# A planner that knows of overlapping VectorE and GpSimd work: a new order for the first block of an H3 and MLP kernel

## The chip, the cores and the metric

The kernel runs on one core of one Trainium2 chip. A core has five engines that run side by side, each with its own queue of instructions, worked off in order: TensorE (PE in the profile; PEld is its weight load), VectorE (DVE), ScalarE (ACT), GpSimd (POOL) and SyncE (SP), which here issues the DMA transfers. Engines wait for one another through semaphores. The metric is the time of one execution on the device in microseconds (us).

## The reference

Two layers of the kind "long convolution, then MLP", both with the same weights, on 2048 tokens of 1024 features. Cut to what is computed:

```python
kv = k_shift * v                      # k_shift: causal convolution of k with 4 taps per channel
kv_f = rfft(pad(kv, 2 * S))           # long causal convolution with ssm_k, by channel
y = irfft(kv_f * rfft(pad(ssm_k)))[:S] + kv * ssm_D
A(q) = q * y
B(x) = square(relu(x @ w1 + b1)) @ w2 + b2      # 1024 -> 3584 -> 1024

x = q
x = x + A(layernorm(x)); x = x + B(layernorm(x))
x = x + A(layernorm(x)); x = x + B(layernorm(x))
```

All is float32. The convolution's result y doesn't depend on x, so it is made once and used in both layers.

## The kernel before, in words

Tokens are cut into four blocks of 512, the convolution into blocks of 256 tokens, which are transformed with tables by TensorE. The frequency products of a block are multiplied element by element, on GpSimd and VectorE, and transformed back. The MLP runs over (layer, block) units in the order of ORDER; every matmul with the weights is made as three matmuls of a high and a low part.

The kernel has two parts. `first_block()` (L932) makes all that the first MLP unit needs, for block 0: for each of 8 groups of 128 channels (c = 0 to 7) the short convolution of k and the product with v (`x_part`, L989), the transform of the filter (`g_part`, L1030), the products and the back transform for the two halves of the block (`prods`, L1127, jj = 0 and 1), the two layer norms (`ln_part`, `tail`), and the first eight weight pieces (`weight`, L1211). What comes after it, from `prod_stream` on, is the steady part: a hand-written loop of MLP steps, into which the convolution of the later blocks is mixed. The change doesn't touch it.

In `first_block` nothing is issued at once. Each operation is a task of a `Plan` (L86): the engines that can take it with a cost in ns for each (`opts`), what it reads and writes, and a latency. `Plan.run` (L177) draws PLAN_TRIES (L42) sets of priorities, the first six plain, then half of them with random factors, the rest as variations of the best so far. For each, `Plan.order` (L124) lays the tasks one after the other on a list of engines: among the tasks that are ready it takes the one that can start earliest, on the engine on which it would end earliest, and it adds that up to an end time. The order with the lowest end time is issued. So the costs decide two things: the order of the instructions on each engine, and, for tasks with two options, which of VectorE (V) and GpSimd (G) takes them.

Tasks with both options are the elementwise ones with inputs in SBUF: the product of the short convolution with v (L997), the frequency products (L1135 for jj = 0, L1140 for jj = 1, with the sum L1142 behind it), the combinations L1146 and L1147, the butterfly (L1149, issued at L655 and L656), the addition to x (L1172), and the low part of a weight (L1218). VectorE alone takes the three remaining steps of the short convolution (L994, a scalar_tensor_tensor), the evictions of transforms from PSUM (L1015, L1054, L1056, L1164, L1207), and the statistics (L1076 to L1096); the normalizations (L1107, L1110) go to VectorE or ScalarE. ScalarE copies the other transforms out. Costs before are straight lines of the number n of elements per partition:

```python
v_cost(n) = 130 + 1.04 * n      # VectorE, no rival on GpSimd
v2_cost(n) = 250 + 1.3 * n      # VectorE, for the tasks that GpSimd could take; +100, +150 or +400 at places
g_cost(n) = 200 + 2.45 * n      # GpSimd
```

Of the kernel before, what the change touches and what calls it, by code (L numbers as in the profile page):

```python
# [19 lines left out]
P = 128  # L20
T = 512
# [6 lines left out]
BL = 256  # L28
# [10 lines left out]
PAIR_GAP = 10  # L39
FWD_WAIT = 4  # L40
PLAN_H = (0.6, 0.7, 0.8, 0.85, 0.9, 0.95)
PLAN_TRIES = 400  # L42
NORM_0 = "VA"
AHEAD_0 = 4
BURST = 1.06
# [40 lines left out]
class Plan:  # L86
# [37 lines left out]
    def order(self, rise, noise):  # L124

        n = len(self.tasks)
        prio = [t[5] - rise * h * z + (1 - rise) * 1000 * i for i, (t, h, z) in enumerate(zip(self.tasks, self.height, noise))]
        waits = [len(t[2]) for t in self.tasks]
        made, left_users = set(), {}
        last = {}  # L130
        for t in self.tasks:
            for x in t[3]:
                left_users[x] = left_users.get(x, 0) + 1
        end, free, seq = [0.0] * n, {}, []
        at = [0.0] * n
        ready = [i for i in range(n) if not waits[i]]
        while ready:
            best = None
            for i in ready:
                opts, _, _, bufs, lat, _ = self.tasks[i]  # L140
                t = at[i]
                ok = True
                for x in bufs:
                    if x not in made:
                        if x.after is not None and x.after not in made or x.prev is not None and left_users[x.prev]:
                            ok = False
                            break
                        if x.prev is not None and last[x.prev] > t:
                            t = last[x.prev]
                if not ok:  # L150
                    continue
                f = None
                for e, c in opts:
                    st = max(t, free.get(e, 0.0))
                    if f is None or st + c < f:
                        f, pick = st + c, (e, c, st)
                key = (pick[2], prio[i])
                if best is None or key < best[0]:
                    best = key, i, pick
            _, i, (e, c, st) = best  # L160
            _, _, _, bufs, lat, _ = self.tasks[i]
            free[e] = st + c
            end[i] = st + c + lat
            for x in bufs:
                made.add(x)
                left_users[x] -= 1
                last[x] = max(last.get(x, 0.0), end[i])
            seq.append((i, e))
            ready.remove(i)
            for j in self.after[i]:  # L170
                waits[j] -= 1
                at[j] = max(at[j], end[i])
                if not waits[j]:
                    ready.append(j)
        return max(end), seq

    def run(self):  # L177
        n = len(self.tasks)
        self.height = [0] * n
        self.after = [[] for _ in range(n)]  # L180
        for i in reversed(range(n)):
            opts, _, deps, _, lat, _ = self.tasks[i]
            self.height[i] += min(c for _, c in opts) + lat
            for d in deps:
                self.height[d] = max(self.height[d], self.height[i])
                self.after[d].append(i)
        rng = np.random.default_rng(1)
        best = None
        for k in range(PLAN_TRIES):
            if k < len(PLAN_H):  # L190
                rise, noise = PLAN_H[k], np.ones(n)
            elif k < PLAN_TRIES // 2:
                rise, noise = PLAN_H[k % len(PLAN_H)], rng.uniform(0.85, 1.15, n)
            else:
                rise, noise = best[2], best[3] * np.where(rng.random(n) < 0.1, rng.uniform(0.7, 1.4, n), 1.0)
            got = self.order(rise, noise.tolist())
            if best is None or got[0] < best[0]:
                best = (*got, rise, noise)
        for i, e in best[1]:
            _, fn, _, bufs, _, _ = self.tasks[i]  # L200
            for x in bufs:
                if x.t is None:
                    x.t = x.make()
            fn(e)
        return best[0]
# [3 lines left out]
    return 130 + 1.04 * n  # L209


def v2_cost(n):
    return 250 + 1.3 * n


def g_cost(n):
    return 200 + 2.45 * n


def a_cost(n):  # L220
# [4 lines left out]
def tile_h3_mlp(ctx: ExitStack, tc: tile.TileContext, q, kT, vT, shk, ssmT, ssmD, w1, b1, w2, b2,  # L225
                fwd_t, pro_t, inv_t, sgn_t, out):
    nc = tc.nc
    V, A, G, PE, SY = nc.vector, nc.scalar, nc.gpsimd, nc.tensor, nc.sync
    ENG = {"V": V, "G": G}
# [702 lines left out]
    def first_block():  # L932
        b = ORDER[0][1]
        pl = Plan()
# [21 lines left out]
        with tc.tile_pool(name="pro", bufs=1) as pro:  # L956
# [32 lines left out]
            def x_part(c, k4, v4):  # L989
                ks = new(cv, "fx", 4, [P, T])  # L990
                pl.add([("A", a_cost(T))], lambda e: A.activation(
                    ks.t, k4.t[:, 3:], AF.Copy, scale=shkt[:, c, 0:1]), [k4], [ks])
                for q_ in range(1, 4):
                    pl.add([("V", v2_cost(T))], lambda e, q_=q_: V.scalar_tensor_tensor(  # L994
                        ks.t, k4.t[:, 3 - q_:T + 3 - q_], shkt[:, c, q_:q_ + 1], ks.t,
                        op0=OP.mult, op1=OP.add), [k4], [ks], lat=130)
                pl.add([("G", g_cost(T)), ("V", v2_cost(T))], lambda e: ENG[e].tensor_mul(  # L997
                    ks.t, ks.t, v4.t), [v4], [ks])
                o = bank("p2", 4, ps2)
                pl.add([("PE", 480)], lambda e: transposes(o.t, ks.t), [ks], [o])  # L1000
                xt = new(cv, "fg", 3, [P, T])
                pl.add([("A", a_cost(T))], lambda e: A.copy(xt.t, o.t), [o], [xt])
                sp = spec["x", c]
                for r in range(2):
                    oi = bank("p2", 4, ps2)

                    def mm(e, r=r, oi=oi):
                        for u in range(2):
                            ou = oi.t[:, u * BL:u * BL + BL]
                            fmm(ou, even(r), xt.t[:, 0:BL], True, False)  # L1010
                            fmm(ou, odd(r, u), xt.t[:, BL:], False, True)
                    pl.add([("PE", 1850)], mm, [xt, *tabs], [oi])
                    pl.add([("A", a_cost(T))], lambda e, r=r, oi=oi: A.copy(spread(sp[r].t), sums(oi.t)), [oi], [sp[r]])
                    if r:
                        pl.add([("V", v_cost(T))], lambda e, oi=oi: V.tensor_add(  # L1015
                            spread(sp[2].t), sums(oi.t), spread(sp[0].t)), [oi, sp[0]], [sp[2]])
                for i in range(3):
                    dma(lambda i=i: dview(XD[i], 0, c), lambda i=i: sp[i].t, [sp[i]])
# [108 lines left out]
            def prods(c, jj):  # L1127
                sm = new(cv, "sm", 2, [P, 3, 2, CU])
                xs, gs = spec["x", c], spec["g", c]
                n = BL * (jj + 1)  # L1130
                for ty, (xi, gi) in enumerate(PAIRS):
                    xt, gt = xs[xi], gs[gi]
                    opts = [("G", g_cost(n)), ("V", v2_cost(n) + 150)]
                    if jj == 0:
                        pl.add(opts, lambda e, ty=ty, xt=xt, gt=gt: ENG[e].tensor_mul(  # L1135
                            sm.t[:, ty], xt.t[:, :, 0], gt.t[:, :, 0]), [xt, gt], [(sm, ty)])
# [1 line left out]
                    pr = new(cv, "fx", 4, [P, T]) if c == KT - 1 else sub("ppr", 3, 512, [P, T], "xl")  # L1138
                    pv = lambda t: t.rearrange("p (g b c) -> p g b c", g=2, b=BT)
                    pl.add(opts, lambda e, xt=xt, gt=gt, pr=pr: ENG[e].tensor_mul(  # L1140
                        pv(pr.t), xt.t, gt.t[:, :, ::-1]), [xt, gt], [pr])
                    pl.add([("V", v2_cost(BL) + 100), ("G", g_cost(BL))], lambda e, ty=ty, pr=pr: ENG[e].tensor_add(  # L1142
                        sm.t[:, ty], pv(pr.t)[:, :, 0], pv(pr.t)[:, :, 1]), [pr], [(sm, ty)])
                two = [("G", g_cost(BL)), ("V", v2_cost(BL) + 100)]
                fl_ = lambda: sm.t.rearrange("p k g c -> p k (g c)")
                pl.add(two, lambda e: ENG[e].tensor_add(fl_()[:, 1], fl_()[:, 0], fl_()[:, 1]), [(sm, 0)], [(sm, 1)])  # L1146
                pl.add(two, lambda e: ENG[e].tensor_sub(fl_()[:, 2], fl_()[:, 0], fl_()[:, 2]), [(sm, 0)], [(sm, 2)])  # L1147
                z = {}
                pl.add([("V", 2 * v2_cost(BL) + 400), ("G", 2 * g_cost(BL))], lambda e: z.update(  # L1149
                    enumerate(butterfly(ENG[e], fl_()))), [], [(sm, 0), (sm, 1), (sm, 2)])  # L1150
                o = bank("pt", 2, pst)

# [9 lines left out]
                for e_ in range(2):  # L1162
                    tt = 2 * jj + e_
# [5 lines left out]
                dma(lambda: YD[0][:, 2 * jj:2 * jj + 2, sl], lambda: yo.t.rearrange("p (e c) -> p e c", e=2), [yo], cost=400)  # L1169
                for e_ in range(2):  # L1170
                    tt = 2 * jj + e_
                    pl.add([("G", g_cost(P)), ("V", v2_cost(P))], lambda e, e_=e_, tt=tt: ENG[e].tensor_add(  # L1172
                        x1[tt].t[:, sl], x1[tt].t[:, sl], yn.t[:, e_]), [(yn, e_)], [(x1[tt], c)])

            tails = {}
# [35 lines left out]
            def weight(w):  # L1211
                _, c, f, kh = wsrc[w]
# [2 lines left out]
                hi, lo = (hl, 0), (hl, 1)  # L1215
                dma(lambda: raw.t, lambda: w1[c * FC + f, :, 4 * kh:4 * kh + 4], w=[raw])
                pl.add([("A", a_cost(512))], lambda e: A.copy(hl.t[:, 0], raw.t), [raw], [hi])
                pl.add([("V", v2_cost(512)), ("G", g_cost(512))], lambda e: ENG[e].tensor_sub(  # L1218
                    hl.t[:, 1], raw.t, hl.t[:, 0].bitcast(F32)), [raw, hi], [lo])
                o = bank("p2", 4, ps2) if kh == 0 else rs[c, f]["b"]  # L1220
                if kh == 0:
# [42 lines left out]
        n = 2 * AHEAD_0  # L1264
# [340 lines left out]
```

## Time and profile before

| | |
|---|---|
| median of 3 runs | 2829.53 us (2827.84 to 2832.18) |
| profiled execution | 2825.19 us |
| its span | 2823.4 us |
| granted TensorE clock, mean | 0.990 |
| DVE busy share in the first 3 of 40 slices | 8, 8, 6 tenths |
| POOL busy share in the first 3 of 40 slices | 6, 8, 2 tenths |
| DMA | 711.71 MB, mean 252 GB/s |

The page cuts the span into 40 slices of 70.6 us; the first block fills the first two. The table of PE's slices has a 7 and an 8 there and 9 in nearly all that follow:

```profile
PE   7899899799999999999999999999999999999999
PEld 6787788688888888888888888888888888888887
DVE  8868688767777877779757654252225322352122
ACT  4254244242334333442234322242224222342222
POOL 6826555345442655336552553001000100001000
```

Each digit is the busy share of a slice in tenths. An instruction that has started counts as busy until it ends, also while it is held up by another engine's use of the memory; so a full DVE or POOL row doesn't say that the engine works all that time.

### The profile page before, as it was taken

Reading aid. Unit: us, or ns where it says so; the run is one execution under the profiler, and the core shown is the slowest. Engines: PE = TensorE matmul, PEld = TensorE weight load, DVE = VectorE, ACT = ScalarE, POOL = GpSimd, SP = SyncE. Lnnn points to the kernel's source line nnn. Section 1 sums busy time; section 2 is a strip of 40 time slices with the busy share of each in tenths; the row PEclk is TensorE's granted clock in tenths of the full one; section 3 lists DMA queues with packets and bytes.
Section 4 is the critical chain, followed back from the end, with each engine's and each line's share of the span. In section 5 each row is a group of like instructions: output and inputs, shape, how many; then the busy total and the mean of one; then the engine's idle time right before and its main releaser. Section 6 shows DMA issues by size and latency. Waiting matters only on the chain.

```text
span 2823.4 us, 35392 instructions
## 1 busy us (share of the span) xinstructions
PE 2751.7 (97%) x12784; PEld 2285.0 (81%) x12784; DVE 1644.8 (58%) x2470; ACT 951.3 (34%) x1649; POOL 922.6 (33%) x644
## 2 busy tenths in 40 slices
PE   7899899799999999999999999999999999999999
PEld 6787788688888888888888888888888888888887
DVE  8868688767777877779757654252225322352122
ACT  4254244242334333442234322242224222342222
POOL 6826555345442655336552553001000100001000
PEclk9899999999999999999999999999999999999999
DMA  8499999789988898888977785475646665575543
GB/s 258 166 302 358 333 327 303 280 264 346 299 282 298 289 335 285 273 323 287 352 250 273 291 310 201 160 270 184 193 146 224 212 205 168 168 264 160 177 146 123
DMA packets 325792, 711.71 MB, mean 252 GB/s; under 512 B 39528, under 2 KB 127728, under 8 KB 325616
## 3 DMA queue, kind: packets, MB, share of 16 engines
q1 hardware_dynamic: 325616, 709.44, 74.0%
q8 instruction: 101, 1.65, 0.2%
q14 instruction: 75, 0.61, 0.1%
HBM read 578.24 MB, written 131.07 MB: 251 GB/s over the span
## 4 chain that ended last, share of the span: by engine, by line
PE 84%; DVE 6%; DMA 5%; POOL 2%; issue 1%; SPq 1%; ACT 0%; DVEq 0%; POOLq 0%; ACTq 0%
PE p L314 26%; PE p L313 26%; PE p L315 26%; DMA cg<-gd 1%; DMA wr<-w 1%; PE pt L314 1%; PE pt L315 1%; PE pt L313 1%; DMA cx<-xd 1%; DVE whl L894 1%; PE p L765 1%; POOL cp L503 1%; PE p L965 1%; DMA wd_m<-whl 0%; PE pt L574 0%
## 5 line engine op out<-in xcount | busy, mean ns | idle before, releaser
L503 POOL TENSOR_TENSOR cp<-cx,cg 128x384 f32<-128x384 f32 (+5 forms) x288 | 539.0, 1884 | 610.1 <-DVE sm L507 360.4
L313 PE MATMUL p<-whl,rh 128*128 128x512 f32 x1792 | 715.1, 399 | 6.7 <-ACT whl L886 3.7
L314 PE MATMUL p<-whl,rh 128*128 128x512 f32 x1792 | 709.9, 396 | 4.3 <-POOL whl L894 2.3
L315 PE MATMUL p<-xh,whl 128*128 128x512 f32 (+1 forms) x1840 | 705.5, 383 | 5.3 <-DVE whl L894 5.3
L315 PE MATMUL p<-whl,rl 128*128 128x512 f32 x1792 | 709.3, 396 | 0.0
L313 PE MATMUL p<-xh,whl 128*128 128x512 f32 (+1 forms) x1840 | 709.0, 385 | 0.1
L314 PE MATMUL p<-xl,whl 128*128 128x512 f32 (+1 forms) x1840 | 705.2, 383 | 0.3 <-DVE xl L1207 0.3
L1291 DVE TENSOR_TENSOR rl<-wr,rh 128x512 fp32r<-128x512 f32 x224 | 193.1, 862 | 582.0 <-ACT rh L1286 581.9
L894 DVE TENSOR_TENSOR whl<-wr,whl 128x512 fp32r<-128x512 f32 x403 | 346.3, 865 | 173.8 <-ACT whl L886 171.4
L886 ACT CAST whl<-wr 128x512 fp32r<-128x512 f32 x410 | 251.2, 618 | 521.0 <-PE p L315 390.0
L1283 ACT ACTIVATE wr<-p,b1t 128x512 f32<-128x512 f32 x222 | 153.2, 690 | 782.1 <-PE p L315 780.9
L313 PEld LDWEIGHTS p<-whl,rh 128*128 128x128 f32 x1792 | 339.1, 189 | 85.9 <-ACT whl L886 4.8
L315 PEld LDWEIGHTS p<-xh,whl 128*128 128x128 f32 x1840 | 348.2, 189 | 73.1 <-DVE whl L894 5.5
L314 PEld LDWEIGHTS p<-whl,rh 128*128 128x128 f32 x1792 | 339.2, 189 | 82.4 <-DVE whl L894 3.1
L315 PEld LDWEIGHTS p<-whl,rl 128*128 128x128 f32 x1792 | 338.8, 189 | 79.7
L313 PEld LDWEIGHTS p<-xh,whl 128*128 128x128 f32 x1840 | 348.5, 189 | 66.3 <-ACT xh L1205 0.3
L314 PEld LDWEIGHTS p<-xl,whl 128*128 128x128 f32 x1840 | 348.3, 189 | 66.0 <-DVE xl L1207 0.5
L1411 POOL TENSOR_TENSOR acc<-acc,px 128x1024 f32<-128x1024 f32 x32 | 84.5, 2673 | 788.4 <-DMA px<-b 777.9
L1297 DVE TENSOR_TENSOR acc<-p,acc 128x512 f32<-128x512 f32 x248 | 167.4, 689 | 254.4 <-PE p L315 253.6
L507 DVE TENSOR_REDUCE sm<-cp 128x128 f32<-128x384 f32 (+5 forms) x288 | 250.1, 875 | 28.7 <-POOL cp L503 25.7
L1284 ACT ACTIVATE wr<-wr 128x512 f32<-128x512 f32 x224 | 141.8, 633 | 7.1
L1286 ACT CAST rh<-wr 128x512 fp32r<-128x512 f32 x224 | 139.2, 621 | 7.1
(192 smaller groups left out, 2141.0 us busy)
## 6 DMA issues: line engine op xcount, KB each, us to landing
whl<-wd_m SPq DMA_DIRECT2D x500, 512.0 KB, 4.1
wr<-w SPq DMA_DIRECT2D x418, 256.0 KB, 4.9
wd_m<-whl SPq DMA_DIRECT2D x70, 512.0 KB, 5.9
cx<-xd SPq DMA_DIRECT2D x48, 512.0 KB, 5.2
cg<-gd SPq DMA_DIRECT2D x48, 512.0 KB, 6.9
gd<-fg SPq DMA_DIRECT2D x72, 256.0 KB, 5.2
cx<-xd SPq DMA_DIRECT2D x48, 384.0 KB, 5.5
cg<-gd SPq DMA_DIRECT2D x48, 384.0 KB, 6.7
```

The source lines that it names most:

```text
L313: PE.matmul(o, lh, rh, start=start, stop=False)
L314: PE.matmul(o, lh, rl, start=False, stop=False)
L315: PE.matmul(o, ll, rh, start=False, stop=stop)
L503: G.tensor_mul(pr.rearrange("p c i -> p i c"), xt[:, 0:j + 1], gt[:, j::-1])
L507: V.tensor_reduce(sm[:, ty, jj], st["pr"], axis=AX.X, op=OP.add)
L886: A.copy(t[:, 0], raws[n]["t"])
L894: ENG[e[n % len(e)]].tensor_sub(t[:, 1], raws[n]["t"], t[:, 0].bitcast(F32))
L1283: A.activation(r, st["o"], AF.Relu, bias=b1t[:, st["f"]:st["f"] + 1])
L1284: A.activation(r, r, AF.Square)
L1286: A.copy(st["hi"], r)
L1291: V.tensor_sub(st["lo"], st["r"]["t"], st["hi"].bitcast(F32))
L1297: V.tensor_add(accs[tt][:, d], o, accs[tt][:, d])
```

## The change

Only the planner's costs and its search change.

- `both(n, k)` gives tasks that either engine can take three numbers for each: the engine, a cost that is now near that of an undisturbed instruction (VectorE 150 + 1.05 n, GpSimd 130 + 2.25 n), and a factor, 0.5. `v2_cost` and its added constants go.
- In `Plan.order` such a task grows by the factor times the time that it overlaps with work of this kind planned earlier on the other of the two engines; `busy` holds until when that is. The growth counts in the choice of the engine too.
- The steps L994 get a cost of 790 with a factor of 0.3, in place of `v2_cost(512)`, which was 916.
- PLAN_TRIES goes from 400 to 800, and with it the point at which the search turns from random sets to variations of the best, from 200 to 400.

```diff
-PLAN_TRIES = 400
+PLAN_TRIES = 800
...
-        end, free, seq = [0.0] * n, {}, []
+        end, free, seq, busy = [0.0] * n, {}, [], {"G": 0.0, "V": 0.0}
...
-                for e, c in opts:
+                for e, c, *port in opts:
                     st = max(t, free.get(e, 0.0))
+                    if port:
+                        c += port[0] * max(0.0, min(busy[e], st + c) - st)
                     if f is None or st + c < f:
-                        f, pick = st + c, (e, c, st)
+                        f, pick = st + c, (e, c, st, port)
...
-            _, i, (e, c, st) = best
+            _, i, (e, c, st, port) = best
+            if port:
+                busy["G" if e == "V" else "V"] = st + c
...
-            self.height[i] += min(c for _, c in opts) + lat
+            self.height[i] += min(o[1] for o in opts) + lat
...
-def v2_cost(n):
-    return 250 + 1.3 * n
...
 def g_cost(n):
-    return 200 + 2.45 * n
+    return 130 + 2.25 * n
+
+
+def both(n, k=1):
+    return [("V", k * (150 + 1.05 * n), 0.5), ("G", k * g_cost(n), 0.5)]
...
-                    pl.add([("V", v2_cost(T))], lambda e, q_=q_: V.scalar_tensor_tensor(
+                    pl.add([("V", 790, 0.3)], lambda e, q_=q_: V.scalar_tensor_tensor(
...
-                pl.add([("G", g_cost(T)), ("V", v2_cost(T))], lambda e: ENG[e].tensor_mul(
+                pl.add(both(T), lambda e: ENG[e].tensor_mul(
...
-                    opts = [("G", g_cost(n)), ("V", v2_cost(n) + 150)]
+                    opts = both(n)
...
-                    pl.add([("V", v2_cost(BL) + 100), ("G", g_cost(BL))], lambda e, ty=ty, pr=pr: ENG[e].tensor_add(
+                    pl.add(both(BL), lambda e, ty=ty, pr=pr: ENG[e].tensor_add(
...
-                two = [("G", g_cost(BL)), ("V", v2_cost(BL) + 100)]
+                two = both(BL)
...
-                pl.add([("V", 2 * v2_cost(BL) + 400), ("G", 2 * g_cost(BL))], lambda e: z.update(
+                pl.add(both(BL, 2), lambda e: z.update(
...
-                    pl.add([("G", g_cost(P)), ("V", v2_cost(P))], lambda e, e_=e_, tt=tt: ENG[e].tensor_add(
+                    pl.add(both(P), lambda e, e_=e_, tt=tt: ENG[e].tensor_add(
...
-                pl.add([("V", v2_cost(512)), ("G", g_cost(512))], lambda e: ENG[e].tensor_sub(
+                pl.add(both(512), lambda e: ENG[e].tensor_sub(
```

Line numbers in the text are those of the kernel before; in the changed one they lie 4 higher from L223 on, less between.

## The prediction

> **What bounds the kernel now.** I read the head of the page first, then the busy time by stage, then the chain of waits around 141 us, and last the timeline of VectorE (DVE) and GpSimd (POOL) inside the first stage.
>
> ```profile
> span 2823.4 us, 35392 instructions
> PE 2751.7 (97%) x12784; PEld 2285.0 (81%) x12784; DVE 1644.8 (58%) x2470; ACT 951.3 (34%) x1649; POOL 922.6 (33%) x644
> ```
>
> The profiled execution took 2825.19 us, 1.8 us around its span, and lies 4.3 us under the median of the three runs (2829.53). Differences below are worked out against the profiled execution and then put on that median. TensorE is busy for 97% of the span, so only stretches where it waits can give time. Busy time by stage (window; length; then PE, PEld, DVE, ACT and POOL, each busy us with its instruction count; clock, DMA share, GB/s):
>
> ```profile
> 0.00:20.00 20.00, 8.47 (x37) 7.52 (x38) 10.97 (x19) 5.21 (x7) 2.41 (x7) 1.00 0.79 270
> 20.00:40.00 20.00, 16.91 (x101) 15.16 (x100) 18.25 (x33) 11.41 (x20) 15.64 (x14) 0.98 0.90 257
> 40.00:130.00 90.00, 79.51 (x465) 71.10 (x464) 82.27 (x137) 26.70 (x51) 84.28 (x90) 0.94 0.60 195
> 130.00:141.64 11.64, 5.34 (x25) 4.41 (x25) 10.73 (x28) 4.70 (x9) 4.74 (x7) 0.64 0.46 173
> 141.64:260.00 118.36, 118.36 (x624) 102.57 (x625) 90.43 (x132) 53.79 (x96) 48.68 (x35) 0.99 0.95 318
> ```
>
> From 141.64 us on PE is busy without a gap. Before it, in 40 to 130 us, DVE is busy 91% and POOL 94%. So the first block is set by these two, and its end is where the chain of waits (start, us, what) hands over to the weight matmuls:
>
> ```profile
> 140.97 0.63 DVE xl L1207
> 141.64 0.54 PE p L314
> ```
>
> Whatever moves that point moves all that follows by as much: from a few us behind it, where the last weights of the block are used, every engine's order is the old one, instruction for instruction, and PE has no idle time that could absorb a shift.
>
> "Busy" on these two engines hides waiting for each other. The timeline (start, us, engine, line, out<-in, count):
>
> ```profile
> 72.17 0.41 DVE L1147 TENSOR_TENSOR sm<-sm 128x256 f32<-128x256 f32 x1
> 125.86 0.28 DVE L1172 TENSOR_TENSOR cg<-cg,fk 128x128 f32<-128x128 f32 x1
> 127.47 1.27 POOL L1140 TENSOR_TENSOR fx<-sx,sg 128x512 f32<-128x512 f32 x1
> 128.78 0.46 POOL L1172 TENSOR_TENSOR cg<-cg,fk 128x128 f32<-128x128 f32 x1
> 129.20 1.26 POOL L1140 TENSOR_TENSOR fx<-sx,sg 128x512 f32<-128x512 f32 x1
> 129.36 1.65 DVE L1140 TENSOR_TENSOR fx<-sx,sg 128x512 f32<-128x512 f32 x1
> 134.03 0.72 POOL L655 TENSOR_TENSOR sm<-sm 128x256 f32<-128x256 f32 x1
> ```
>
> DVE's product L1140 at 129.36 started 0.16 us behind POOL's and ended at 131.01, 0.55 us after POOL's had ended at 130.46: it waited for it, then ran. Undisturbed times are therefore the shortest records: DVE 0.41 us for 256 elements and 0.28 for 128; POOL 0.72, 0.46 and 1.27 for 256, 128 and 512. For DVE's 512 the start of the block has 0.69 (L997), and 0.73 for L994's three-operand form:
>
> ```profile
> 6.38 1.54 DVE L994 SCALAR_TENSOR_TENSOR fx<-xh,shkt,fx 128x512 f32<-128x512 f32 x2 [5.52 <-ACT fx L991]
> 8.96 3.07 DVE L994 SCALAR_TENSOR_TENSOR fx<-xh,shkt,fx 128x512 f32<-128x512 f32 x3
> 12.34 0.73 DVE L994 SCALAR_TENSOR_TENSOR fx<-xh,shkt,fx 128x512 f32<-128x512 f32 x1
> 13.11 0.69 DVE L997 TENSOR_TENSOR fx<-fx 128x512 f32<-128x512 f32 x1
> 9.77 1.71 POOL L997 TENSOR_TENSOR fx<-fx 128x512 f32<-128x512 f32 x1 [8.46 <-DVE fx L994]
> ```
>
> **The change part by part.** The tasks of the first block are the same 627; only their order and, for those that DVE or POOL can take, the engine differ. The new costs, the overlap term and the 800 tries act on the host alone; each costs nothing on the chip except through the order that they select.
>
> *Moved between the engines.* In the new order POOL has 87 elementwise operations instead of 110. To DVE go 28 of 256 elements (11 butterflies, L655 and L656, make 22; L1146 4; L1147 and L1142 one each) and one of 512 (L997). To POOL go two of 256 (L1135), two of 512 (L1140, L1218) and two of 128 (L1172). With the undisturbed times:
> POOL: -28 x 0.72 - 1.27 + 2 x 0.72 + 2 x 1.27 + 2 x 0.46 = -16.5 us.
> DVE: +28 x 0.41 + 0.69 - 2 x 0.41 - 2 x 0.69 - 2 x 0.28 = +9.4 us.
> If the two exclude each other and one of them always has such work pending, the stage shortens by the sum, -7.1 us. That is the end in the kernel's favour.
>
> The other end comes from DVE's own queue. Groups of DVE instructions from 0 to 145 us (line, op, tiles, count; busy us, mean ns; idle before), first those with both inputs in SBUF, then those that read PSUM or one tensor:
>
> ```profile
> L994 DVE SCALAR_TENSOR_TENSOR fx<-xh,shkt,fx 128x512 f32<-128x512 f32 x24 | 22.7, 952 | 6.3 <-ACT fx L991 6.2
> L1140 DVE TENSOR_TENSOR xl<-sx,sg 128x512 f32<-128x512 f32 x7 | 7.3, 1043 | 0.0
> L1147 DVE TENSOR_TENSOR sm<-sm 128x256 f32<-128x256 f32 x8 | 7.3, 910 | 1.9 <-POOL sm L1135 1.3 <-POOL sm L1142 0.6
> L1135 DVE TENSOR_TENSOR sm<-sx,sg 128x256 f32<-128x256 f32 x10 | 7.2, 729 | 0.8 <-PE pt L965 0.8
> L1146 DVE TENSOR_TENSOR sm<-sm 128x256 f32<-128x256 f32 x8 | 6.7, 854 | 0.7 <-POOL sm L1142 0.7
> L997 DVE TENSOR_TENSOR fx<-fx 128x512 f32<-128x512 f32 x5 | 5.9, 1189 | 0.0
> L1142 DVE TENSOR_TENSOR sm<-xl 128x256 f32<-128x256 f32 x8 | 5.4, 670 | 0.0
> L1172 DVE TENSOR_TENSOR cx<-cx,fk 128x128 f32<-128x128 f32 x10 | 5.1, 514 | 0.0
> L1172 DVE TENSOR_TENSOR cg<-cg,fk 128x128 f32<-128x128 f32 x9 | 4.7, 527 | 0.0
> ...
> L1164 DVE SCALAR_TENSOR_TENSOR fk<-pt,cp 128x128 f32<-128x128 f32 x24 | 6.4, 278 | 3.2 <-PE pt L965 2.3 <-ACT fx L1167 0.9
> L1015 DVE TENSOR_TENSOR sx<-p,sx 128x512 f32<-128x512 f32 x8 | 5.4, 677 | 3.1 <-ACT sx L1013 3.1
> L1054 DVE TENSOR_TENSOR sg<-p,sg 128x512 f32<-128x512 f32 x8 | 5.4, 676 | 0.0
> L1056 DVE TENSOR_TENSOR sg<-p,sg 128x512 f32<-128x512 f32 x8 | 5.4, 675 | 0.0
> L1076 DVE BATCH_NORM_STATS2 st<-cg 128x6 f32<-128x512 f32 x8 | 5.4, 683 | 0.3 <-POOL cg L1172 0.3
> L1076 DVE BATCH_NORM_STATS2 st<-cx 128x6 f32<-128x512 f32 x8 | 5.4, 670 | 0.0
> L1164 DVE SCALAR_TENSOR_TENSOR fk<-pt,px 128x128 f32<-128x128 f32 x8 | 2.2, 280 | 0.2 <-PE pt L965 0.2
> ```
>
> The first nine groups last longer than undisturbed by 5.3 + 2.5 + 4.0 + 3.2 + 3.6 + 2.5 + 2.1 + 2.3 + 2.2 = 27.7 us (24 x (0.952 - 0.73) for the first, and so on), 0.25 us for each of POOL's 110 operations. The last seven, 35.6 us, are as long as undisturbed: they run while POOL works, and cover it. If each operation left on POOL holds DVE up by 0.25 us as now, 23 fewer save 5.8 us and DVE's own time grows by 9.4: +3.6 us, the end against it.
>
> I choose between by the row of 40 to 130 us. POOL works or waits for 84.28 of 90 us there, so 6% of DVE's plain work is uncovered. Without 16.5 us it would hold 67.8 us of about 83, and 18% is uncovered. Of the 35.6 us about 25 lie there (an estimate by length: 90 of the 128 us from 13 us, where such work begins, to the end of the block). Uncovered work grows from 1.5 to 4.6 us, 3.1 us lost. The term is -7.1 + 3.1 = **-4.0 us**, with ends -7.1 and +3.6.
>
> A rule speaks to the first end. The Trainium skill, page "SBUF — State Buffer", section "Who interferes with whom", says that a VectorE instruction with two SBUF inputs and a GpSimd instruction that reads SBUF exclude each other, the later one blocked until the earlier ends. The pair at 129.2 us agrees (1.65 us where 0.69 is undisturbed). By that rule alone the term would be -7.1; the plan's new cost charges half of an overlap. I keep -4.0, since uncovered work is no matter of the lock.
>
> *The start of the block.* Now DVE makes two of the three L994 steps of the first channel group, turns to L1032 for a load, makes the third at 8.96, and POOL's L997 ends at 11.48. In the new order the three steps stand together and L997 follows on DVE: 6.38 + 1.54 + 0.73 + 0.69 = 9.34 us, 2.1 earlier, if the loads behind it are there. SP issues the two tables ahead of the second group's keys, so they come no later in the queue. But the second group's keys do, and the 20 to 40 us stage shows DVE busy for 18.25 of 20 us, so not all of it passes on. Ends 0 and -2.1; I take **-1.5 us**, since the chain there runs from this L997 through TensorE to the first products.
>
> *Cross waits, other queues.* The waits on SP and ACT (DMA share 0.60, ACT 26.70 of 90 us in the middle) keep room for another order; I take zero, and the ends above hold what they could cost. What is late next if DVE queues up: the evictions L1015, L1054 and L1056 stand behind the added butterflies, and PE's next transforms wait for their banks; PE has 10 us free in the middle stage.
>
> Sum: -4.0 - 1.5 = **-5.5 us**: 2819.7 for the profiled execution, **2824.0** on the median. Ends: -9.2 and +3.6, that is 2820.3 and 2833.1.
>
> **The rivals.** *The whole saving passes on.* POOL keeps something pending because the search now sees overlap; then -7.1 - 1.5 to -2.1, about **2820.5**. For it speaks the 94% of POOL in the middle; against it that POOL loses 16.5 us of work and so must run dry more often.
>
> *The exchange is even.* DVE pays in its own time what it saves in waiting: +3.6 - 1.5 = +2.1, **2831.6**, and between that and the forecast lies no change at all. For it speaks DVE's 91%. The Trainium skill, "Perfetto Trace Analysis", section "Optimizing Scalar/DVE Operations", warns that shifting work between these two engines might not help, as they share a port; the trace's 27.7 us of stretched instructions is what it means, though here work goes to the quicker user.
>
> *DVE becomes the bound (slower).* Fewer POOL operations, but the waiting on DVE does not shrink, because the products left on POOL are its long ones (1.27 us). Then +9.4 - 1.5 = +7.9, **2837.4**. It decides from 0.29 us of waiting for each of POOL's 87 operations ((27.7 + 5.7 - 7.9) / 87) against 0.25 now. Against it: the shorter chains of three operations on one engine need fewer crossings.
>
> That the change does nothing is excluded by the 23 operations that move; that the end stays because the last chain sets it is part of the even case.
>
> **How the numbers follow.** 0.2%, 5.7 us, is about what a measurement here can tell from no change. Forecast (-2 to -7.5 us) 0.47, whole saving 0.23, even 0.18, DVE the bound 0.12. The forecast lies on the threshold, so nearly half of it counts as faster: 0.22 + 0.23 = 0.45 faster; 0.25 + 0.18 = 0.43 within; 0.12 slower. The range goes to both ends of the sum, 2819.5 to 2833.5; it leaves the slower case out. The forecast's own range is 2822 to 2827.5.
>
> **What would show it.** Right: the hand-over L1207 to L314 near 136 us instead of 141.64; POOL near 69 us of undisturbed work, its share in the middle near 80%; the first L997 on DVE ending near 9.4 us; PE without a gap behind the hand-over. Wrong: mean times of L994, L1146 and L1147 on DVE above 0.95, 0.85 and 0.91 us; idle DVE in the middle above 8 us; or a shift at 141 us that the end of the span does not show.

## The result and the profile after

| | before | changed |
|---|---|---|
| median (19 executions each) | 2829.53 us | 2833.19 us |
| lowest to highest | 2826.37 to 2834.05 | 2826.28 to 2838.9 |
| ratio, 95% interval | | 1.0014, [1.0008, 1.0020] |
| hand-over, in the profiled execution | 141.64 us | 144.96 us |

The changed kernel is 4.0 us slower (0.0014 x 2829.5), between 2.3 and 5.7 us. The forecast was 5.5 us faster; the nearest case was the even exchange (2831.6). The median lies 0.3 us inside the slow end of the stated range (2833.5); the range was wide enough to take in the wrong direction, and that is no credit to the working. The profiled execution took 2832.4 us, 7.2 us over the profiled one of before. Single executions of one kernel lie up to 12.6 us apart, so that difference says little; below I compare medians, and the hand-over inside the profiles. Line numbers of the changed kernel lie 4 higher here: L314 is now L318, L994 is L998, L1164 is L1168.

The head of the page of the changed kernel:

```profile
span 2830.6 us, 35391 instructions
PE 2749.4 (97%) x12784; PEld 2284.6 (81%) x12784; DVE 1654.5 (58%) x2493; ACT 951.2 (34%) x1649; POOL 904.1 (32%) x621
```

POOL has 23 operations fewer and 18.5 us less busy time, DVE 23 more and 9.7 us more. The counts are those that were read from the order. Of DVE's 9.7 us only 3.0 lie ahead of the hand-over, as the rows further down show; the rest lies behind it, where the instructions didn't change and DVE's busy time differs from profile to profile anyway (1522.6 us in the one of before, 1525.6 in its repeat, 1529.3 here, 1519 to 1532 over all kernels below).

Busy time by stage of the changed kernel (window; length; PE, PEld, DVE, ACT, POOL, each busy us with its count; clock, DMA share, GB/s):

```profile
0.00:20.00 20.00, 10.31 (x43) 8.93 (x44) 9.91 (x17) 5.68 (x8) 1.98 (x7) 1.00 0.81 266
20.00:40.00 20.00, 18.36 (x112) 16.48 (x112) 18.47 (x44) 10.09 (x18) 16.12 (x18) 1.00 0.90 285
40.00:130.00 90.00, 74.20 (x444) 67.27 (x443) 85.35 (x147) 27.07 (x53) 65.08 (x65) 0.94 0.57 190
130.00:144.96 14.96, 6.74 (x34) 5.61 (x33) 11.46 (x34) 4.71 (x10) 3.51 (x5) 0.64 0.41 156
144.96:260.00 115.04, 113.49 (x603) 98.21 (x603) 88.69 (x128) 52.72 (x93) 47.36 (x34) 0.99 0.90 307
```

The first 40 us went better than before: PE did 28.67 us of work there (10.31 + 18.36), against 25.38. In the middle stage this turns round. POOL is busy for 72% (65.08 of 90) instead of 94%, DVE for 95% instead of 91%, and PE for 74.20 us instead of 79.51. Of these 5.3 us PE had done 3.3 earlier; at 130 us it is 2.0 us of work behind.

PE around the hand-over, from the timeline (start, us, engine, line, operands, count, idle before):

```profile
144.09 0.76 PE L1204 MATMUL p<-ident,cp 128*128 128x128 f32 x4 [0.53 <-DVE xl L1211]
144.50 0.56 PE L317 MATMUL p<-xh,whl 128*128 128x256 f32 x1
144.96 0.58 PE L318 MATMUL p<-xl,whl 128*128 128x256 f32 x1
```

The first matmul with the low part xl, which stood at 141.64 us, stands at 144.96. The time was lost ahead of this point, 3.3 us, and the medians differ by 3.7.

To see of what the 3.3 us consist, I split the time up to the hand-over into three parts of DVE. *Idle* is the hand-over less DVE's busy time, both from one row of the stage view. *Own* is what DVE's instructions take undisturbed: their counts times the step from one start to the next, 0.34 us for 256 elements, 0.60 to 0.62 for 512, 0.67 for L994's form, 0.21 for 128 (records of neighbours overlap by some 0.07 us). *Wait* is busy less own. POOL's own time is likewise its counts times 0.69, 1.24 and 0.42 us. The two rows, before and changed:

```profile
0.00:141.64 141.64, 110.23 (x625) 98.19 (x625) 122.23 (x215) 48.02 (x87) 107.08 (x116) 0.93 0.66 212
```
```profile
0.00:144.96 144.96, 109.61 (x626) 98.28 (x626) 125.19 (x239) 47.56 (x87) 86.68 (x93) 0.93 0.63 210
```

Before: own 81.3, wait 40.9, idle 19.4. Changed: own 89.4, wait 35.8, idle 19.8. So own time grew by 8.1 us, waiting fell by 5.1, idle time rose by 0.4. Busy and idle time are measured; how busy time divides into own and waiting hangs on the steps. With the median steps of the kernel that leaves POOL empty (below), own time is 80.6 and 87.8, so it grows by 7.2 us and waiting falls by 4.2. The differences of the split are good to about 1 us, and busy time rises by 3.0 us either way.

Where the waiting went shows in the groups of DVE instructions from 0 to 145 us of the changed kernel (count; busy us, mean ns; idle before):

```profile
L998 DVE SCALAR_TENSOR_TENSOR fx<-xh,shkt,fx 128x512 f32<-128x512 f32 x24 | 21.4, 894 | 7.5 <-ACT fx L995 7.4
L660 DVE TENSOR_TENSOR sm<-sm 128x256 f32<-128x256 f32 x13 | 9.1, 698 | 0.4
L659 DVE TENSOR_TENSOR sm<-sm 128x256 f32<-128x256 f32 x13 | 8.4, 649 | 0.1
L1151 DVE TENSOR_TENSOR sm<-sm 128x256 f32<-128x256 f32 x9 | 8.0, 891 | 0.0
L1150 DVE TENSOR_TENSOR sm<-sm 128x256 f32<-128x256 f32 x12 | 7.6, 632 | 0.0
L1144 DVE TENSOR_TENSOR xl<-sx,sg 128x512 f32<-128x512 f32 x7 | 6.3, 917 | 0.0
L1139 DVE TENSOR_TENSOR sm<-sx,sg 128x256 f32<-128x256 f32 x8 | 5.3, 685 | 0.0
L1001 DVE TENSOR_TENSOR fx<-fx 128x512 f32<-128x512 f32 x6 | 5.1, 858 | 0.0
L1176 DVE TENSOR_TENSOR cx<-cx,fk 128x128 f32<-128x128 f32 x9 | 5.0, 555 | 0.0
L1146 DVE TENSOR_TENSOR sm<-xl 128x256 f32<-128x256 f32 x8 | 4.3, 546 | 0.0
L1176 DVE TENSOR_TENSOR cg<-cg,fk 128x128 f32<-128x128 f32 x8 | 3.4, 430 | 0.0
```

The nine groups that the prediction counted are now longer than undisturbed by 20.5 us instead of 27.7 (24 x (0.894 - 0.73) = 3.9 for the first, and so on). But the 26 butterfly operations L659 and L660, which were 4 on DVE before, bring stretches of 6.8 us themselves (13 x (0.698 - 0.41) + 13 x (0.649 - 0.41)). Together 27.3 us. The work that was moved to the quicker engine waits there too. Of the four of before, the two of L655 were undisturbed (0.409 us), and the two of L656 stretched by 1.4 us (2 x (1.110 - 0.41)):

```profile
L656 DVE TENSOR_TENSOR sm<-sm 128x256 f32<-128x256 f32 x2 | 2.2, 1110 | 0.1
```

### The profile page after: what moved, and what is told of

The parts are those of the page before. It is cut to its first block, busy times and chain, and to the rows that moved or that the text cites. A ratio compares the mean times of both kernels' runs of the same rounds, so it can differ in the third digit from the quotient of the medians.

```text
span 2830.6 us, 35391 instructions
## 1 busy us (share of the span) xinstructions
PE 2749.4 (97%) x12784; PEld 2284.6 (81%) x12784; DVE 1654.5 (58%) x2493; ACT 951.2 (34%) x1649; POOL 904.1 (32%) x621
## 4 chain that ended last, share of the span: by engine, by line
PE 83%; DVE 8%; DMA 6%; issue 1%; POOL 1%; ACT 1%; SPq 1%; DVEq 0%; POOLq 0%; ACTq 0%
PE p L318 26%; PE p L317 26%; PE p L319 26%; DMA cg<-gd 1%; DMA wd_m<-whl 1%; DMA wr<-w 1%; PE pt L318 1%; PE pt L319 1%; PE pt L317 1%; PE p L969 1%; PE p L769 1%; DVE whl L898 1%; DMA xd<-fy 1%; DVE sm L511 1%; POOL cp L507 0%
## 5 line engine op out<-in xcount | busy, mean ns | idle before, releaser
L318 PE MATMUL p<-whl,rh 128*128 128x512 f32 x1792 | 708.6, 395 | 4.0 <-POOL whl L898 2.1
L318 PE MATMUL p<-xl,whl 128*128 128x512 f32 (+1 forms) x1840 | 705.9, 384 | 0.0
L318 PEld LDWEIGHTS p<-whl,rh 128*128 128x128 f32 x1792 | 338.4, 189 | 81.7 <-DVE whl L898 2.8
L318 PEld LDWEIGHTS p<-xl,whl 128*128 128x128 f32 x1840 | 348.7, 189 | 65.6 <-DVE xl L1211 0.2
```

What stands on the lines that cost most here:

```text
L318: PE.matmul(o, lh, rl, start=False, stop=False)
```

## The experiments

The experiments change only how the planner chooses, or give it the engines or the whole order outright; what is computed stays the same. Where an interval is given, the kernel was timed several times. The others were executed once, under the profiler; of those I use the hand-over and the split, since one execution says little about the median.

### Engines and order apart

The changed kernel's order, with the 78 tasks that changed engine put back on the engine of before:

```diff
+ON_G = {517, 391, 392,
...
+ON_V = {265, 143, 401,
...
-            fn(e)
+            fn("G" if i in ON_G else "V" if i in ON_V else e)
```

> The changed order of tasks, but each of the 78 tasks that changed between VectorE and GpSimd is given back to the engine that it had before (110 operations on GpSimd again). Theory A, the exchange of engines decides (VectorE's own time against its waiting): own time back to about 82 us from 89, waiting back to about 41 us from 36, hand-over of the first block at 141 to 143 us, the kernel within 2 us of before. Theory B, the order itself decides (TensorE's stalls at 50 to 60 us and a longer tail): the hand-over stays at 144.5 us or later, the kernel 3 to 5 us slower than before.

And the reverse: the order of before, with the changed kernel's engines for these 78 (the same edit on the kernel before, with the two sets exchanged).

> The order of tasks of before, with the engines that the changed plan chose for the same 78 tasks (87 operations on GpSimd). Theory A: VectorE's own time about 90 us, waiting 33 to 36 us, hand-over at 143 to 145 us, the kernel 2 to 4 us slower than before. Theory B: hand-over at 141 to 142 us, the kernel as before.

The stage rows up to the hand-over, first the new order with old engines, then the old order with new engines:

```profile
0.00:149.39 149.39, 113.73 (x626) 100.90 (x626) 116.64 (x217) 47.13 (x86) 99.97 (x116) 0.90 0.62 204
```
```profile
0.00:145.39 145.39, 110.95 (x625) 98.51 (x625) 124.66 (x238) 48.04 (x87) 84.19 (x93) 0.93 0.64 208
```

New order, old engines: 2838.47 us, 1.0037 [1.0024, 1.0051], hand-over at 149.39. DVE is busy 116.64 us and idle 32.7, 13 more than before. Two of DVE's waits in it (what waited, for what: us, times, longest); the longest wait of DVE for POOL in the kernel before was 1.3 us:

```profile
DVE sm L1153 <- POOL sm L1141: 2.5, 1, 2.5
DVE sm L1148 <- POOL xl L1146: 2.3, 1, 2.3
```

By the count above own time is about 81 us again, as the first theory has it, but waiting is about 36 us and not 41, and the kernel is slower than either theory said. An order made for one assignment leaves holes when it is run with another, so this run doesn't price the order by itself.

Old order, new engines: 2832.89 us, 1.0009 [1.0000, 1.0017], hand-over at 145.39, 3.75 us later than before: own 89.1 (+7.8), wait 35.6 (-5.3), idle 20.7 (+1.3). This is nearly the split of the changed kernel, without its order. So the exchange of engines is enough for the rise in DVE's busy time, and for a hand-over as late as that of the whole change. The whole time agrees, but its interval (0 to 4.8 us) reaches down to no change. The two runs don't add up to the change (7.7 and 3.7 us against 3.3), so order and engines can't be priced apart.

### No GpSimd at all

```diff
 def both(n, k=1):
-    return [("V", k * (150 + 1.05 * n), 0.5), ("G", k * g_cost(n), 0.5)]
+    return [("V", k * (150 + 1.05 * n), 0.5)]
```

> The changed planner, but the tasks that either engine could take go to VectorE alone; GpSimd has none in the first block. Theory A (instructions on VectorE are stretched only by GpSimd holding the memory port): no stretched instruction is left, 256-element ones 0.41 us in the mean, waiting 0 to 2 us; own time 121 us, and with the 19.5 us of idle time that both kernels show the hand-over at 140 to 143 us, about as before, with no GpSimd at all. Rival (the stretch has another cause, DMA or ScalarE): waiting stays near 30 us and the hand-over is at 165 us or later.

Measured: 2838.93 us, 1.0029 [1.0019, 1.0040]. The groups of DVE up to 149 us, and its row up to the hand-over:

```profile
L998 DVE SCALAR_TENSOR_TENSOR fx<-xh,shkt,fx 128x512 f32<-128x512 f32 x24 | 17.7, 746 | 0.0
L660 DVE TENSOR_TENSOR sm<-sm 128x256 f32<-128x256 f32 x16 | 6.8, 425 | 0.6
L1151 DVE TENSOR_TENSOR sm<-sm 128x256 f32<-128x256 f32 x16 | 6.7, 419 | 0.0
L659 DVE TENSOR_TENSOR sm<-sm 128x256 f32<-128x256 f32 x16 | 6.7, 416 | 0.0
L1150 DVE TENSOR_TENSOR sm<-sm 128x256 f32<-128x256 f32 x16 | 6.6, 418 | 0.0
```
```profile
0.00:148.79 148.79, 112.23 (x625) 100.40 (x626) 121.17 (x319) 47.15 (x86) 0.70 (x6) 0.89 0.63 205
```

With POOL empty, 256 elements take 0.42 us in these four groups instead of 0.63 to 0.89, and 512 in three-operand form 0.746 instead of 0.894; the wait falls to 0.8 us (121.17 - 120.4; 2.5 by the second count). ScalarE and the DMA queues, the rivals named above, worked on: ACT is busy for 47.15 us (47.56 in the changed kernel), and the DMA share is 0.63 in both. So the stretch comes from POOL's work. The hand-over is another matter: it came at 148.79 us, not at 140 to 143. The Trainium skill, "SBUF — State Buffer", "Who interferes with whom", calls the shared port an exclusive lock; the means of 0.42 us with POOL empty against 0.63 to 0.89 agree.

The same row holds the main lesson of this study: DVE is busy for 121.17 us with 104 more instructions than before, and for 122.23 us in the kernel before, where POOL did 85.5 us of that work. POOL's help took nothing off DVE's busy time; that is even 1 us longer with it. What this kernel loses against before is idle time, 27.6 us instead of 19.4. Its order is another one too, so this run doesn't tell how much of that comes from the empty POOL. Its longest waits of DVE:

```profile
DVE fk L1168 <- ACT xl L1171: 12.3, 7, 4.6
DVE xh L1036 <- DMA xh<-ssmT: 6.4, 1, 6.4
```

### The costs and the number of tries apart

New costs with the old number of tries; old costs with the new number; the overlap charged in full; and the kernel before once more, for the scatter of one profile:

```diff
-PLAN_TRIES = 800
+PLAN_TRIES = 400
```

> The changed kernel with 400 tries. GpSimd has 90 operations, VectorE 90 us of own time, as with 800. If the costs are what moves the work and the time: hand-over 143 to 148 us. If the longer search did it: 141 to 142 us.

```diff
-PLAN_TRIES = 400
+PLAN_TRIES = 800
```

> The kernel before with 800 tries. GpSimd keeps 111 operations, VectorE 82 us of own time. If the costs are what moves the time: hand-over at 141 to 143 us. If more tries lead to an order that is worse on the chip: 144 us or later.

```diff
-    return [("V", k * (150 + 1.05 * n), 0.5), ("G", k * g_cost(n), 0.5)]
+    return [("V", k * (150 + 1.05 * n), 1.0), ("G", k * g_cost(n), 1.0)]
...
-                    pl.add([("V", 790, 0.3)], lambda e, q_=q_: V.scalar_tensor_tensor(
+                    pl.add([("V", 790, 1.0)], lambda e, q_=q_: V.scalar_tensor_tensor(
```

> The changed kernel with a factor of 1.0 for every overlap in place of 0.5 and 0.3. GpSimd has 78 operations (62 us), VectorE 94 us of own time. Waiting at 0.41 us for each: 94 + 32 + 19.5, hand-over at 145 to 146 us, as with 0.5. If the too low factor is what misled the search: waiting below 28 us and the hand-over at 141 us or earlier.

> The kernel before once more, unchanged, on this chip: how far the hand-over repeats. If it is set by the order: 141.6 us within 0.5. If executions differ: more.

Each search draws its random factors from a fixed seed. Three further runs draw them from another one: old costs with 400 tries, new costs with 800, new costs with 400.

```diff
-        rng = np.random.default_rng(1)
+        rng = np.random.default_rng(2)
```

> The kernel before, its random priorities from another seed; GpSimd 111 operations, VectorE 82 us of own time. If the costs decide: hand-over at 140 to 143 us. If the order of before was a lucky one of many that its planner holds for equal: 144 us or later.

> The changed kernel, its random priorities from another seed; GpSimd 89 operations, VectorE 90 us of own time. If the costs decide: hand-over at 143 to 147 us. If the order of the changed kernel was an unlucky one: 142 us or earlier.

> The changed kernel with 400 tries and the other seed; GpSimd 87 operations, VectorE 92 us of own time. If the price of the exchange is in the costs and the idle time is chance: VectorE busy (own and waiting) 124 to 127 us as in the three others with the new costs, idle anywhere from 15 to 22, hand-over 139 to 148 us. If the longer search is what hurts: hand-over at 141 to 142 us, as with the first seed at 400 tries.

The split of each in us, from its row of the stage view up to its hand-over as above:

| kernel | hand-over | DVE busy | own | wait | idle | POOL own | this execution |
|---|---|---|---|---|---|---|---|
| old costs, 400 (before) | 141.6 | 122.2 | 81.3 | 40.9 | 19.4 | 85.5 | 2825.2 |
| the same again | 142.3 | 121.1 | 81.3 | 39.8 | 21.2 | 85.5 | 2833.1 |
| old costs, 400, other seed | 142.4 | 120.1 | 81.8 | 38.3 | 22.3 | 84.1 | 2829.4 |
| old costs, 800 | 143.9 | 122.1 | 81.2 | 40.9 | 21.7 | 85.1 | 2832.5 |
| new costs, 400 | 141.3 | 126.0 | 90.0 | 36.0 | 15.3 | 69.3 | 2829.1 |
| new costs, 400, other seed | 142.3 | 126.1 | 91.3 | 34.8 | 16.2 | 66.6 | 2837.2 |
| new costs, 800 (changed) | 145.0 | 125.2 | 89.4 | 35.8 | 19.8 | 69.7 | 2832.4 |
| new costs, 800, other seed | 146.9 | 124.9 | 89.1 | 35.8 | 22.0 | 69.1 | 2834.8 |
| overlap in full, 800 | 141.2 | 123.6 | 93.5 | 30.1 | 17.6 | 61.3 | 2830.6 |

The rows of the two kernels with new costs and 400 tries, the second with the other seed:

```profile
0.00:141.28 141.28, 110.00 (x625) 99.15 (x626) 125.95 (x237) 47.66 (x86) 84.78 (x96) 0.93 0.67 215
0.00:142.28 142.28, 110.40 (x626) 99.41 (x626) 126.05 (x240) 47.01 (x86) 85.00 (x93) 0.91 0.64 213
```

Three things follow. The new costs make DVE busier in all four profiles, 124.9 to 126.1 us against 120.1 to 122.2; the groups don't touch, and one kernel's own repeat moved DVE's busy time by 1.1 us and the hand-over by 0.7. Second, with 400 tries the new costs also leave less idle time (15.3, 16.2), and then the hand-over is about where it was. Third, with 800 tries that gain is gone with either seed (19.8, 22.0), and the hand-over is 3.7 and 4.6 us later. So with these two seeds the 800 orders are part of the loss. Why they do worse stays open: it is two seeds, and I made no run that tells a misled search from chance. The old costs show less of it, 143.9 us with 800 tries against 141.6 to 142.4 with 400. What can be said is that a longer search doesn't have to help on the chip: it takes the lowest planned end, and the planned end needn't follow DVE's real waits. Charging the overlap in full gave the earliest hand-over among the 800s, 141.2 us, with 30.1 us of waiting, between the 32 and the 28 that the two theories gave; that is one execution with one seed.

### A planner with the lock, and an order from replayed queues

In the planner the two engines exclude each other, with 0.06 us of overlap (HANDOVER, 60 ns), at undisturbed costs; the steps L998 get 670 in place of 790 and are held to the same rule:

```diff
-                        c += port[0] * max(0.0, min(busy[e], st + c) - st)
+                        st = max(st, lock[e])
...
-                busy["G" if e == "V" else "V"] = st + c
+                lock["G" if e == "V" else "V"] = st + c - HANDOVER
...
-    return [("V", k * (150 + 1.05 * n), 0.5), ("G", k * g_cost(n), 0.5)]
+    return [("V", k * (70 + 1.05 * n), 1), ("G", k * g_cost(n), 1)]
```

> The planner treats the port as exclusive: a task with inputs in SBUF on one engine cannot start until the other engine's has ended (less 60 ns), where the changed kernel lengthens it by half of the overlap. It leaves 36 operations on GpSimd and gives VectorE 108 us of own time. If waiting costs 0.4 us for each operation on GpSimd whatever the order: 108 + 15 + 19.5, hand-over at 143 us, no faster than before. If an order can put VectorE's plain work (evictions, statistics, 35 us) under GpSimd's operations: waiting 2 to 7 us, hand-over at 130 to 135 us, 6 to 11 us faster than before.

Measured: 2835.84 us, 1.0021 [1.0011, 1.0031], hand-over 145.85. This planner leaves 36 operations on POOL:

```profile
0.00:145.85 145.85, 107.85 (x626) 97.02 (x626) 125.64 (x289) 48.24 (x88) 37.59 (x42) 0.93 0.64 209
```

DVE's own time is 107.7 us, so it waits 17.9 us for 31.5 us of POOL's work, 57%. Waiting and hand-over lie near the theory of a fixed price for each operation (15 us, 143 us), and far from the other (2 to 7 us, 130 to 135). The plan, by its construction, has no overlap beyond 0.06 us for each; 17.9 us of waiting mean that the queues stood otherwise on the chip than in the plan. My reading, which no run singles out, is that a right rule in the planner isn't enough if its clock is off.

The last kernel therefore gives `Plan` a finished order (and engine) for the 627 tasks, in place of the search:

```diff
+ORDER_0 = [0, 3, 7, 2, 4, 1, 37, 38, 8,
...
+        best = 0.0, [(i, "GVADP"[k] if k < 4 else "PE") for i, k in zip(ORDER_0, map(int, ENGINE_0))]
```

It was found by replaying orders through in-order queues with the durations of these traces: DVE and POOL one at a time, readers of one PSUM tile one after the other. Such a replay is fitted and proves nothing. The measurement shows what its order is worth, not that the lock alone makes it so, since the replay also has other durations and a rule for PSUM.

> The same 627 tasks, in an order written out as a list. It was chosen, outside the kernel, by replaying the five queues with durations from the traces of the six kernels so far, with the port held by one engine at a time and with engines that read the same PSUM bank one after the other. It leaves 39 operations (30 us) on GpSimd and gives VectorE 109 us of own time. Theory A (VectorE's time to the hand-over is own + waiting + idle, and only covered work on GpSimd gains): waiting 6 to 12 us, idle 16 to 20, hand-over at 133 to 138 us, 4 to 8 us faster than before. Rival (GpSimd's work always costs VectorE half a microsecond each, as in the planner with an exclusive port): 109 + 19 + 19.5, hand-over at 147 us, slower than both.

Measured: 2821.33 us (9 executions) against 2830.04 before, 0.9967 [0.9956, 0.9979]: 9.3 us faster than before, and so ahead of both kernels. The row up to the hand-over, and the chain of waits there:

```profile
0.00:134.38 134.38, 106.75 (x625) 95.55 (x625) 119.57 (x288) 48.36 (x88) 36.60 (x46) 0.95 0.69 227
```
```profile
134.38 0.58 PE p L326
```

Own 108.4, wait 11.2, idle 14.8; POOL's 40 operations are 30.4 us, of which DVE waits for 37%. The timeline shows how (L1009 is the product with v, L1066 and L1068 are evictions from PSUM, L1147 a frequency product):

```profile
59.32 1.46 POOL L1009 TENSOR_TENSOR fx<-fx 128x512 f32<-128x512 f32 x1
59.56 0.68 DVE L1068 TENSOR_TENSOR sg<-p,sg 128x512 f32<-128x512 f32 x1
60.16 0.67 DVE L1066 TENSOR_TENSOR sg<-p,sg 128x512 f32<-128x512 f32 x1
60.96 0.74 DVE L1147 TENSOR_TENSOR sm<-sx,sg 128x256 f32<-128x256 f32 x2
```

POOL's 512 product lies over two evictions that keep their undisturbed 0.68 us, and the next DVE pair with both inputs in SBUF starts at 60.96, after POOL's end at 60.78. Against the planner with the lock the gain in this kernel is 11.5 us at the hand-over: 6.7 of wait and 5.4 of idle, less 0.7 more of own time. Against the kernel before it is 7.3 us: 2.7 of DVE's busy time (119.57 against 122.23) and 4.6 of idle time. So the larger part of what it wins over before is idle time, not work that POOL took over; which of the order's moves won it, no run tells.

### Does a shift at the hand-over reach the end?

| kernel | hand-over against 141.64 | whole time, 95% interval |
|---|---|---|
| changed | +3.3 | +2.3 to +5.7 |
| new order, old engines | +7.7 | +6.8 to +14.4 |
| old order, new engines | +3.7 | 0 to +4.8 |
| no GpSimd | +7.1 | +5.4 to +11.3 |
| planner with the lock | +4.2 | +3.1 to +8.8 |
| order from replay | -7.3 | -12.5 to -5.9 |

The last column is the ratio's interval times 2829.5. All six shifts lie inside their intervals, so the runs agree with this: what happens ahead of the hand-over is paid once, in full, whatever its sign. The intervals are 3.4 to 7.6 us wide, and the base, 141.64 us, came at 142.34 in its repeat, so a part of a shift could be lost unseen.

The prediction gave as the reason that PE has no idle time behind the hand-over. Its row shows this up to 260 us; from the hand-over to the end of the span PE is idle for 40.3 us in the kernel before and 45.8 in the changed one, so there was room, and it is the runs that speak for a full shift.

The part behind the hand-over also scatters by more than most of these shifts. From there to the end of the span the kernel before took 2681.8 us in the first profile and 2689.0 in the repeat, the changed one 2685.6. The longest, 2693.1, is that of new costs with 400 tries and the other seed, which took 2837.2 us though its hand-over came at 142.3. This is why the single executions are not compared by their whole time.

## Why the prediction was wrong

**Right.** The hand-over is the point that counts; the six rows above agree with it. POOL kept 69.7 us of undisturbed work; 69 was said. The start went as described: L997 (now L1001) runs on DVE right behind the three steps and ends at 9.55 us, against 9.34 predicted. The chain of the changed kernel:

```profile
8.85 0.70 DVE fx L1001
9.69 1.10 PE p L402 x4
10.79 8.23 PE p L969 x32
19.66 0.69 DVE sx L1019
```

**The start's gain was given back.** The term of -1.5 us took it that an early start reaches the end. DVE's idle time to the hand-over is 19.8 us against 19.4, so it didn't stay. One place where it may have gone, in the chain of the changed kernel, from 51.8 us on:

```profile
51.82 1.71 PE pt L969 x8
53.53 4.62 PE p L969 x16
58.15 0.91 PE pt L969 x8
59.12 0.39 ACT xl L1171
59.54 0.29 DVE fk L1168
```

The chain goes there through TensorE's transforms and ScalarE's copy to DVE, which waits 3.3 us for that copy in two waits between 40 and 70 us; before, it had no wait there but one of 0.6 us. I can't say which of the changed places in the order caused it; the split shows only that the idle time as a whole came back.

**The step that failed** is the choice of -4.0 us between the ends -7.1 and +3.6. DVE's busy time up to the hand-over rose by 3.0 us (8.1 of own, less 5.1 of waiting), so the truth is at the end against the change. That end used 5.8 us of waiting saved and 9.4 of own time added: both were near, though the nine groups held only 27.7 of the 40.9 us of waiting.

The reason given for the choice was POOL's share of the middle stage: if POOL's work falls from 94% to about 82%, only the plain DVE work that is left uncovered is lost. This fails twice. The share fell to 72%. And the -7.1 us at its root took it that DVE's waiting falls by all of POOL's removed 16.5 us (+9.4 - 16.5); it fell by 5.1. My reading is that what counts is not how much of the stage POOL works, but how much of POOL's work lies under DVE instructions that don't need the port, and DVE had 23 more operations that do. (The 28 and 1 operations of the prediction, less the 6 that go back, are net by line; 45 tasks left POOL and 33 came to it.) So of each us of POOL's own work DVE waited 0.48 us before (40.9 / 85.5) and 0.51 after (35.8 / 69.7). The 15.8 us of POOL work that were taken away gave back only 0.32 us each (5.1 / 15.8), and cost 0.51 us each on DVE (8.1 / 15.8). By the second count these are 0.27 and 0.46 us. The exchange would have paid only if about half of the removed POOL time or more had been waited for.

**The rivals.** The even exchange had the right mechanism, and is nearest at 2831.6; it was short by the 1.5 us of the start, which it also kept. For "DVE becomes the bound" I had set 0.29 us of stretched time for each POOL operation as the point of decision. By that count, 27.3 us over 87 operations, it came to 0.31. It still cost less than the 7.9 us given. DVE's own time grew by 8.1 us and not by 9.4, and the waiting, which this case kept as it was, fell by 5.1 us: by 1.8 in these groups with the butterflies (27.7 + 1.4 - 27.3), by the rest outside them.

**The signs that I named.** Three of those for being right were missing: the hand-over came at 144.96 us and not near 136, POOL's share of the middle was 72% and not near 80%, and PE has a gap behind the hand-over, 1.55 us in the row of 144.96 to 260 us, where it waits for DVE. The signs for being wrong were poor ones. The mean times of L994, L1146 and L1147 (0.894, 0.632, 0.891 us) stayed under the bounds, and DVE's idle time in the middle stage was 4.65 us (90 less 85.35), under the 8 named, so neither gave a warning. The waiting had moved to the butterflies, a group that wasn't on the list. The sum over all groups would have shown it.

The warning of the Trainium skill, page "Perfetto Trace Analysis", section "Optimizing Scalar/DVE Operations", that shifting work between these two engines might not help, fits: old order with new engines is 1.0009 [1.0000, 1.0017].

## What to carry to other kernels

When two engines exclude each other, split the time of the one that bounds into own time, waiting and idle time, and price a move by the waiting that it *saves*, not by the waiting there is on average: here 0.32 us saved for each us of POOL work against 0.51 us added. Look for an order that places the slower engine's work under instructions of the other that don't need the shared port, in the real queues' time: here DVE waited for 37% of POOL's work in the order from replay, and for 42 to 57% in the other orders. Watch the idle time as well, which made the larger part of the best order's gain. A longer search over a plan doesn't have to end earlier on the chip; compare plans at the point that they are to move, here the hand-over, over more than one seed.

## What was unexpected in the hardware

DVE's busy time up to the hand-over was 121.2 us with nothing of this work on POOL, 119.6 with 30.4 us of it, 125.6 with 31.5, 125.2 with 69.7 and 122.2 with 85.5: it doesn't fall as POOL takes over more. The lowest value, 116.6 with 85.5, is that of the new order with old engines, where DVE was idle the longest. By DVE's busy time two engines at one port did about as much as one alone.

With POOL empty, DVE's longest waits were for ScalarE's copy L1171, which reads the same `pt` tile that DVE's L1168 reads: 12.3 us in 7 waits. Whether the program's semaphores alone put these two readers in turn, or the bank would too, no run here tells.
